# Attention before two MLPs on one core: one or two chunks of p times v made from rounded parts

## The chip, the cores and the metric

The kernel runs on one core of a Trainium2 chip. The metric is device time in microseconds (us) of one execution. Engines are named as in the profile: PE is TensorE (PEld its weight loads), DVE is VectorE, ACT is ScalarE, POOL is GpSimd, SP is SyncE. The time before is the median of three runs, 1681.91 us (1679.18 to 1683.67).

## The reference

Three stages run one after the other on 4 batches of 448 tokens. Attention has 12 heads of 64 elements; two MLPs of width 768 and 3072 follow, the second behind a mix of the tokens through U and V.

```python
q_n, k_n = (rmsnorm(q, g_q), rmsnorm(k, g_k))
scores = 1/sqrt(64) * matmul(q_n, k_n.T)
scores = scores - max(scores, axis=-1)
attn = exp(scores)
attn = attn / (sum(attn, axis=-1) + 1e-09)
x = matmul(attn, v)                       # heads side by side: 4 x 448 x 768
xn = (x - mean) / sqrt(var + 1e-06) * g_ln
x = x + relu(xn @ w_ch1) @ w_ch2          # first MLP
u = x + ((x.T @ U) @ V).T                 # mix of tokens
out = u + relu(u @ w2_ch1) @ w2_ch2       # second MLP
```

## The kernel before

The 48 heads (4 batches of 12) go through `attention` one after the other, two heads of a pair sharing the preparation. The 448 tokens are cut into `NC` = 4 chunks of `CP` = 112. One turn of the main loop is a head, and a turn has four slots, one for each chunk. In a slot every task that is under way makes one step, in the order of `OS`: `sc` (scores of head i, exponentials), `mx` (maxima of head i+2), `pv` (p times v of head i-1), `t1` (transposes of k and q of head i+3, tiles `pk` and `pq`), `t2` (transposes with the maximum, `pt`) and `norm`. Between them run generators in the background: `pre` (norms and rounded parts of q and k, a pair ahead), `pre_v` (loads v), `load_uv`, `scale` (division by the sum of p), `ln_stats` and `ln_apply` (the LayerNorm of a batch whose 12 heads are done; for batches 0 and 1 within attention) and, from head 38 on, `early` and `late` (first weights of the MLP). A scheduler sets the final order on each engine, except for what `pin` holds in its order; every engine then works through its own list without overtaking.

fp32 numbers reach the faster matmul as parts: `F32R` is a rounded fp32 that TensorE takes in one pass, and a product of two split numbers is made as high times high, low times high and high times low. A matmul with plain `F32` operands takes two records in the trace.

`sc` multiplies twice per chunk (L475, L476) into a bank `ps`, and ScalarE writes p, 112x448, as `pf` tile of type F32 (L479). `pv` multiplies p by `vf` (L500): v's 64 columns, and ones behind them up to 128, so that row 64 of the result `po` is the sum of p. VectorE copies the 65 rows that are wanted (L514). The constant `NX` = 4 = `NC` makes all four chunks F32; the branches for rounded parts exist but are not taken, and `pre_v` ends after its two loads of `vf`.

In `mx` VectorE reduces each chunk of scores to its maxima straight from a PSUM bank (L450). Seven banks of tag "ps" go round among `ps`, `pm`, `po` and the transposes. `pre` on GpSimd: multiplication by the norm's factors (L300, twice), low part of k (`kk`, L305), low part of q (`ql`, L308), and the gains (`later`, L287). `kk` of a pair is read by `pk` of `t1` (L428). LayerNorm on GpSimd: L184 and L219 subtract the mean, L215 makes the low part; on VectorE: L163 sums, L181, L222; `scale` multiplies at L555.

Of the kernel before, what the change touches and what calls it, by code (L numbers as in the profile page):

```python
# [8 lines left out]
F32 = mybir.dt.float32  # L9
F32R = mybir.dt.float32r  # L10
# [3 lines left out]
AF = mybir.ActivationFunctionType  # L14
ALU = mybir.AluOpType
AX = mybir.AxisListType

B, H, S, D = 4, 12, 448, 64
P = 128
CP = 112  # L20
NC = S // CP
DM = H * D
DFF = 4 * DM
KD = DM // P
# [6 lines left out]
NWF = 5  # L31
NP0 = 2
EPS = 1e-6
NX = 4
OS = "smpabn"
QW = D + 2
HL = 8
PVY = (0, 1, 2)
# [5 lines left out]
def f32(ap):  # L44
    return ap.bitcast(F32)


def build(tc, qkv, gg, g_ln, w1a, w2a, w1b, w2b, u_in, v_in, out):
    nc = tc.nc
    V, A, PL, PE = nc.vector, nc.scalar, nc.gpsimd, nc.tensor  # L50
    with ExitStack() as es:
# [9 lines left out]
        def bank(name, tag=None):  # L61
            cnt[0] += 1
            tag = tag or banks["tag"]
            return banks["pool"].tile([P, 512], F32, tag=tag, name=f"{name}{cnt[0]}", bufs=banks[tag])
# [40 lines left out]
        v4 = const([4 * R, S], F32R, "v4")  # L105

        def load_ggt(tp):
            gsb = tp.tile([CP, 2, D], F32, tag="gsb", name="gsb")
            nc.scalar.dma_start(gsb, gg)
            ggt = tp.tile([CP, D], F32, tag="ggt", name="ggt")  # L110
            V.scalar_tensor_tensor(ggt, gsb[:, 0, :], 1.0 / D ** 0.5, gsb[:, 1, :], ALU.mult, ALU.mult)
            return ggt
# [22 lines left out]
        x = [xpool.tile([P, KD, S], F32, tag=f"x{b}", name=f"x{b}") for b in range(B)]  # L135
        xh = [npool.tile([P, KD, S], F32R, tag=f"xh{j}", name=f"xh{j}") for j in range(2)]
        xl = [npool.tile([P, KD, S], F32R, tag=f"xl{j}", name=f"xl{j}") for j in range(2)]
# [4 lines left out]
        def pin(ins):  # L142
            return tc.keep_in_program_order(ins) if pins[0] else ins
# [82 lines left out]
        def attention(ap, ep, ep2, early, late):  # L226
            NH = B * H
            NP = NH // 2
            kks, vfs, vhs, vls, a2s = [], [], [], [], []
            st = {}  # L230
# [13 lines left out]
            pre_load(0)  # L244
            side["ln"] = bank("ln", "ln")
            ggt = load_ggt(ap)
            identr = ap.tile([CP, CP], F32R, tag="identr", name="identr")
            pin(V.tensor_copy(identr, ident[:CP, :CP]))
# [2 lines left out]
                PE.matmul(warm[:, :P], ones_m, ones_m, start=True, stop=True)  # L251
            later = ap.tile([CP, D], F32, tag="later", name="later")
            for i in range(2):
                for lst, nm, dt, one in ((vfs, "vf", F32, 1.0), (vhs, "vh", F32R, 1.0), (vls, "vl", F32R, 0.0)):
                    n = NX if nm == "vf" else NC - NX
                    if n == 0:
                        lst.append(None)
                        continue
                    t = ap.tile([CP, 2, n, P], dt, tag=f"{nm}{i}", name=f"{nm}{i}")
                    PL.memset(f32(t[:, :, :, D:P]), one)  # L260
                    lst.append(t)
            for i in range(NA2):
                t = ap.tile([P, S], F32R, tag=f"a2{i}", name=f"a2{i}")
                PL.memset(f32(t[D:QW, :]), 1.0)
                a2s.append(t)
            qls = []
            for i in range(3):
                t = ep.tile([CP, 2 * NC, QW], F32R, tag=f"ql{i}", name=f"ql{i}")
# [133 lines left out]
            def pre_v(pr):  # L402
                b, hp = divmod(pr, H // 2)
                v = qkv[b, hp, :, 2].rearrange("p (j c) d -> p j c d", j=2)
                for j in range(2):
                    ins = (nc.scalar if pr else nc.sync).dma_start(vfs[pr % 2][:, j, :, 0:D], v[:, j, 0:NX])
                    if pr:
                        pin(ins)
                if NX == NC:
                    return  # L410
                vr = ap.tile([CP, 2, NC - NX, D], F32, tag="vr", name=f"vr{pr}", bufs=2)
                nc.sync.dma_start(vr, v[:, :, NX:])
                yield
                yield
                yield
                vh, vl = vhs[pr % 2], vls[pr % 2]
                for j in range(2):
                    A.copy(vh[:, j, :, 0:D], vr[:, j])
                yield
                for j in range(2):  # L420
                    PL.tensor_tensor(vl[:, j, :, 0:D], vr[:, j], f32(vh[:, j, :, 0:D]), ALU.subtract)

            def t1(n):
                pr, j = divmod(n, 2)
# [43 lines left out]
            def sc(n):  # L468
                a1, bq, a2 = st.pop(("ab", n))
                t = st.pop(("t2", n))  # L470
                st["p", n] = ps = []
                for c in range(NC):
                    pb = bank("ps")
                    cs = slice(c * CP, (c + 1) * CP)
                    PE.matmul(pb[:CP, :S], a1[:, cs], bq, start=True, stop=False)  # L475
                    PE.matmul(pb[:CP, :S], a2[:QW, cs], t[:QW], start=False, stop=True)  # L476
                    if c < NX:
                        p = ap.tile([CP, S], F32, tag="pf", name=f"p{n}_{c}", bufs=NX + 2)
                        A.activation(p, pb[:CP, :S], AF.Exp)  # L479
                        ps.append(p)  # L480
                    else:
                        p = ap.tile([CP, S], F32, tag="p", name=f"p{n}_{c}", bufs=2)
                        ph = ap.tile([CP, S], F32R, tag="ph", name=f"ph{n}_{c}", bufs=NC - NX + 1)
                        pl = ap.tile([CP, S], F32R, tag="pl", name=f"pl{n}_{c}", bufs=NC - NX + 1)
                        A.activation(p, pb[:CP, :S], AF.Exp)
                        V.tensor_copy(ph, p)
                        PL.tensor_tensor(pl, p, f32(ph), ALU.subtract)
                        ps.append((ph, pl))
                    if c < NC - 1:
                        yield  # L490

            def pv(n):
                pr, j = divmod(n, 2)
                ps = st.pop(("p", n))
                vf, vh, vl = vfs[pr % 2], vhs[pr % 2], vls[pr % 2]
                po = bank("po")
                st["po", n] = po
                for c in range(NC):
                    if c < NX:
                        PE.matmul(po[:, :S], vf[:, j, c, :], ps[c], start=(c == 0), stop=(c == NC - 1))  # L500
                    else:
                        ph, pl = ps[c]
                        PE.matmul(po[:, :S], vh[:, j, c - NX, :], ph, start=(c == 0), stop=False)
                        PE.matmul(po[:, :S], vl[:, j, c - NX, :], ph, start=False, stop=False)
                        PE.matmul(po[:, :S], vh[:, j, c - NX, :], pl, start=False, stop=(c == NC - 1))
                    if c in PVY:
                        yield

            def norm(n):
# [56 lines left out]
            for i in range(-3 - T1, NH + 2):  # L566
                def ok(n):
                    return 0 <= n < NH
                if i == -3 - T1:
                    start = first_two()  # L570
# [13 lines left out]
                if i - 2 in (H, 2 * H, 3 * H):  # L584
                    b = (i - 2) // H - 1
# [29 lines left out]
        bufs, held, rings, ready = {}, {}, {}, {}  # L615
# [890 lines left out]
```

## Time and profile before

| | us |
|---|---|
| three runs, median | 1681.91 |
| profiled execution | 1675.09 |
| its span | 1673.3 |
| PE busy | 1661.3 |
| DVE, ACT, POOL busy | 1203.5, 1000.5, 1051.1 |

The profiled execution is a run of its own, 1.8 us longer than its span, and shorter than the median of the three timed runs. The first matmul of the MLPs starts at 338.3 us; before that lies attention. Matmuls are pipelined and their ends are modelled: of matmuls in a row, the distances of their starts tell more than one's length, and a busy PE isn't yet a PE at its peak. A window view gives for each engine the busy time in a stretch.

### The profile page before, as it was taken

What the parts mean: (1) busy time and instruction counts of PE and PEld (TensorE: products, weight loads), DVE (VectorE), ACT (ScalarE), POOL (GpSimd) and SP (SyncE); (2) the same over time, 40 slices, a digit from 0 to 9 for tenths busy, and PEclk for the clock granted to TensorE, in tenths of its full rate; (3) what the DMA queues carried; (4) which work ended last, traced back from release to release, by engine and by line L of the source; (5) the groups of instructions that cost most, each with busy time, mean ns of one, the idle gap of its engine ahead of it and who ended that gap; (6) DMA issues with size and microseconds to landing.
All of it is one profiled execution on the core that took longest, in us unless ns stands there. A gap on an engine that the chain in (4) does not pass through costs nothing.

```text
span 1673.3 us, 24654 instructions
## 1 busy us (share of the span) xinstructions
PE 1661.3 (99%) x8223; PEld 1460.3 (87%) x8223; DVE 1203.5 (72%) x1913; ACT 1000.5 (60%) x2098; POOL 1051.1 (63%) x924
## 2 busy tenths in 40 slices
PE   8999999999999999999999999999999999999999
PEld 6666666689999999999999999999999999999998
DVE  6657777879897887866767686657667854565665
ACT  7877888867878876544544455444445534454541
POOL 5446767559767787755655687555555655776752
PEclk8999999999999999999999999999999999999999
DMA  3435444766755566544445427565657463444432
GB/s 98 117 83 128 121 117 136 205 223 207 236 178 174 185 207 202 190 139 131 152 136 159 157 85 255 190 221 176 226 189 250 166 207 118 147 151 123 150 124 76
DMA packets 134430, 273.39 MB, mean 163 GB/s; under 512 B 37280, under 2 KB 57664, under 8 KB 134304
## 3 DMA queue, kind: packets, MB, share of 16 engines
q1 hardware_dynamic: 112252, 265.24, 49.8%
q10 hardware_dynamic: 22052, 6.59, 1.7%
q8 instruction: 65, 1.06, 0.3%
q14 instruction: 61, 0.50, 0.1%
HBM read 178.80 MB, written 81.96 MB: 156 GB/s over the span
## 4 chain that ended last, share of the span: by engine, by line
PE 94%; DVE 2%; DMA 1%; POOL 1%; issue 1%; ACT 1%; SPq 0%; POOLq 0%; DVEq 0%; ACTq 0%
PE bank L1111 35%; PE bank L1289 33%; PE po L500 7%; PE bank L1233 6%; PE ps L475 2%; PE b L1111 2%; PE pm L449 2%; PE ps L476 2%; PE b L1233 2%; PE t L978 1%; PE pk L428 1%; PE pq L436 1%; PE xt L968 1%; PE pt L463 0%; DMA xl<-rs 0%
## 5 line engine op out<-in xcount | busy, mean ns | idle before, releaser
L1289 PE MATMUL bank<-h,w 128*128 128x448 f32 x2655 | 586.1, 366 | 0.0
L1289 PEld LDWEIGHTS bank<-h,w 128*128 128x128 f32 x2655 | 498.3, 188 | 38.3 <-issue 0.4
L1300 DVE TENSOR_TENSOR x<-x,bank 128x448 f32<-128x448 f32 x450 | 275.8, 616 | 188.8 <-PE bank L1289 183.8
L1111 PE MATMUL bank<-xh,w 128*128 128x448 f32 x1158 | 330.5, 367 | 0.0
L785 POOL TENSOR_TENSOR w<-wf,w 128x384 fp32r<-128x384 f32 x201 | 222.7, 1119 | 133.1 <-ACT w L784 131.6
L785 POOL TENSOR_TENSOR w<-s,w 128x384 fp32r<-128x384 f32 x151 | 173.4, 1151 | 152.4 <-ACT w L784 149.1
L1111 PE MATMUL bank<-T,w 128*128 128x448 f32 x1134 | 251.9, 367 | 0.0
L1111 PEld LDWEIGHTS bank<-xh,w 128*128 128x128 f32 x1158 | 217.2, 188 | 17.5 <-issue 0.7
L1111 PEld LDWEIGHTS bank<-T,w 128*128 128x128 f32 x1134 | 212.3, 188 | 16.4
L1111 PE MATMUL bank<-xl,w 128*128 128x448 f32 x579 | 211.9, 366 | 0.0
L784 ACT CAST w<-s 128x384 fp32r<-128x384 f32 x151 | 77.1, 515 | 174.5 <-PE bank L1111 160.5
L500 PE MATMUL po<-p,vf 112*128 112x448 f32 x384 | 175.6, 539 | 0.2 <-DVE m L450 0.2
L450 DVE TENSOR_REDUCE m<-pm 112x1 f32<-112x448 f32 x192 | 118.5, 619 | 64.4 <-PE pm L449 63.8
L784 ACT CAST w<-wf 128x384 fp32r<-128x384 f32 x201 | 101.5, 514 | 100.6 <-PE bank L1111 81.7
L83 DVE SCALAR_TENSOR_TENSOR wf<-wf,raw 128x384 uint32<-128x384 uint32 x180 | 135.2, 757 | 13.2 <-ACT raw L71 5.3
L785 POOL TENSOR_TENSOR w<-raw,w 128x384 fp32r<-128x384 f32 x72 | 81.9, 1154 | 57.1 <-ACT w L784 57.0
L1111 PEld LDWEIGHTS bank<-xl,w 128*128 128x128 f32 x579 | 108.9, 188 | 8.6
L79 ACT ACTIVATE wf<-raw 128x384 f32<-128x384 f32 x180 | 99.3, 553 | 27.5 <-DMA raw<-in_w2a 11.2
L479 ACT ACTIVATE p<-ps 112x448 f32<-112x448 f32 x192 | 104.5, 546 | 4.3 <-PE ps L476 2.1
L1103 DVE SCALAR_TENSOR_TENSOR h<-tm,h 128x448 fp32r<-128x448 f32 x103 | 99.7, 968 | 2.9 <-ACT h L1102 2.2
L71 ACT ACTIVATE raw<-raw 128x384 uint32<-128x384 uint8 x180 | 100.0, 558 | 0.0
L475 PE MATMUL ps<-bq,a 128*112 128x448 f32 x192 | 98.6, 513 | 0.0
(263 smaller groups left out, 2891.1 us busy)
## 6 DMA issues: line engine op xcount, KB each, us to landing
wd<-wf SPq DMA_DIRECT2D x94, 384.0 KB
ws<-w SPq DMA_DIRECT2D x84, 384.0 KB
w<-ws SPq DMA_DIRECT2D x84, 384.0 KB
wf<-wd SPq DMA_DIRECT2D x51, 384.0 KB
raw<-wd SPq DMA_DIRECT2D x48, 384.0 KB
raw<-in_w1b SPq DMA_DIRECT2D x48, 384.0 KB
raw<-in_w2b SPq DMA_DIRECT2D x48, 384.0 KB
raw<-in_w2a SPq DMA_DIRECT2D x44, 384.0 KB
```

The lines of the kernel that those rows point to most:

```text
L71: A.activation(r[:, :, 0], r.bitcast(U8).rearrange("p n (t q) -> p n t q", t=2)[:, :, 0, 3], AF.Copy, scale=1.0 / 32, bias=-31.0 / 64)
L83: V.scalar_tensor_tensor(f, f, 3, r[:, :, 0], ALU.logical_shift_left, ALU.bitwise_or)
L450: V.tensor_reduce(m[:, c:c + 1], pm[:CP, :S], AX.X, ALU.max)
L475: PE.matmul(pb[:CP, :S], a1[:, cs], bq, start=True, stop=False)
L479: A.activation(p, pb[:CP, :S], AF.Exp)
L500: PE.matmul(po[:, :S], vf[:, j, c, :], ps[c], start=(c == 0), stop=(c == NC - 1))
L784: job(A, 520, lambda: A.copy(form(key)[0], src()), ins, ("hi",) + key, [key])
L785: job(PL, 1100, lambda: PL.tensor_tensor(form(key)[1], src(), f32(form(key)[0]), ALU.subtract), [("hi",) + key], key, rel=rel)
L1111: PE.matmul(out[:, :S], wt[:, k, :], xt[:, k, :], start=(first and n == 0), stop=(last and n == 8), skip_group_check=True)
L1233: PE.matmul(at(*to)[:, :S], wt[:, e, :], xt, start=(m in "13" and n == 0), stop=(n == 2), skip_group_check=True)
L1289: PE.matmul(at(*key)[:, :S], wt[:, e % 3, :], t, start=(n == 0), stop=(n == 3 * G - 1))
L1300: V.tensor_tensor(x[b][:, e, :], x[b][:, e, :], at(*key)[:, :S], ALU.add)
```

## The change

`NX` goes, and four numbers come: `H0, H2, H1, NV = 4, 14, 38, 2`. `parts(n)` says how many chunks of head n are made from rounded parts: none in heads 0 to 3, two in heads 4 to 13, one in heads 14 to 37, none from 38 on. All four chunks of v stay in `vf` as F32, now 66 columns wide (`QW`), and `vh` and `vl` hold the high and low part of the first one or two. For such a chunk VectorE writes the high part of p as a maximum over an axis of one element (`ph`), GpSimd subtracts (`pl`), two slots after the exponential; `pv` takes the F32 chunks first and the rounded ones last, with three matmuls each. `ph` and `pl` live in slices of `xh[1]` and `xl[1]` up to head 23 and in the MLP's weight ring `w` from 24 on. The first load `gsb` goes to a corner of `x[3]`.

```diff
@@ -31,7 +31,7 @@
 NWF = 5
 NP0 = 2
 EPS = 1e-6
-NX = 4
+H0, H2, H1, NV = 4, 14, 38, 2
 OS = "smpabn"
 QW = D + 2
 HL = 8
@@ -105,7 +105,7 @@
         v4 = const([4 * R, S], F32R, "v4")
 
         def load_ggt(tp):
-            gsb = tp.tile([CP, 2, D], F32, tag="gsb", name="gsb")
+            gsb = x[B - 1][:CP, 0, :2 * D].rearrange("p (j d) -> p j d", j=2)
             nc.scalar.dma_start(gsb, gg)
             ggt = tp.tile([CP, D], F32, tag="ggt", name="ggt")
             V.scalar_tensor_tensor(ggt, gsb[:, 0, :], 1.0 / D ** 0.5, gsb[:, 1, :], ALU.mult, ALU.mult)
@@ -251,14 +251,23 @@
                 PE.matmul(warm[:, :P], ones_m, ones_m, start=True, stop=True)
             later = ap.tile([CP, D], F32, tag="later", name="later")
             for i in range(2):
-                for lst, nm, dt, one in ((vfs, "vf", F32, 1.0), (vhs, "vh", F32R, 1.0), (vls, "vl", F32R, 0.0)):
-                    n = NX if nm == "vf" else NC - NX
-                    if n == 0:
-                        lst.append(None)
-                        continue
-                    t = ap.tile([CP, 2, n, P], dt, tag=f"{nm}{i}", name=f"{nm}{i}")
-                    PL.memset(f32(t[:, :, :, D:P]), one)
+                for lst, nm, dt, n, one in ((vfs, "vf", F32, NC, 1.0), (vhs, "vh", F32R, NV, 1.0), (vls, "vl", F32R, NV, 0.0)):
+                    t = ap.tile([CP, 2, n, QW], dt, tag=f"{nm}{i}", name=f"{nm}{i}")
+                    PL.memset(f32(t[:, :, :, D:QW]), one)
                     lst.append(t)
+            spare = [xx[1][:CP, k, :] for xx in (xh, xl) for k in range(KD)]
+            ring_w = [t.rearrange("p a b c -> p (a b c)")[:CP, :S] for t in bufs["w"]]
+            taken = [0]
+
+            def parts(n):
+                return 0 if n < H0 else NV if n < H2 else 1 if n < H1 else 0
+
+            def homes(n):
+                pool = spare if n < 2 * H else ring_w
+                i = taken[0] % len(pool)
+                taken[0] += 2
+                return pool[i], pool[i + 1]
+
             for i in range(NA2):
                 t = ap.tile([P, S], F32R, tag=f"a2{i}", name=f"a2{i}")
                 PL.memset(f32(t[D:QW, :]), 1.0)
@@ -402,23 +411,20 @@
             def pre_v(pr):
                 b, hp = divmod(pr, H // 2)
                 v = qkv[b, hp, :, 2].rearrange("p (j c) d -> p j c d", j=2)
+                vf, vh, vl = vfs[pr % 2], vhs[pr % 2], vls[pr % 2]
                 for j in range(2):
-                    ins = (nc.scalar if pr else nc.sync).dma_start(vfs[pr % 2][:, j, :, 0:D], v[:, j, 0:NX])
+                    ins = (nc.scalar if pr else nc.sync).dma_start(vf[:, j, :, 0:D], v[:, j])
                     if pr:
                         pin(ins)
-                if NX == NC:
+                m = parts(2 * pr)
+                if m == 0:
                     return
-                vr = ap.tile([CP, 2, NC - NX, D], F32, tag="vr", name=f"vr{pr}", bufs=2)
-                nc.sync.dma_start(vr, v[:, :, NX:])
-                yield
-                yield
-                yield
-                vh, vl = vhs[pr % 2], vls[pr % 2]
-                for j in range(2):
-                    A.copy(vh[:, j, :, 0:D], vr[:, j])
-                yield
-                for j in range(2):
-                    PL.tensor_tensor(vl[:, j, :, 0:D], vr[:, j], f32(vh[:, j, :, 0:D]), ALU.subtract)
+                yield
+                yield
+                yield
+                A.copy(vh[:, :, :m, 0:D], vf[:, :, :m, 0:D])
+                yield
+                PL.tensor_tensor(vl[:, :, :m, 0:D], vf[:, :, :m, 0:D], f32(vh[:, :, :m, 0:D]), ALU.subtract)
 
             def t1(n):
                 pr, j = divmod(n, 2)
@@ -469,41 +475,44 @@
                 a1, bq, a2 = st.pop(("ab", n))
                 t = st.pop(("t2", n))
                 st["p", n] = ps = []
+                st["hl", n] = hl = []
+
+                def part(c):
+                    ph, pl = homes(n)
+                    V.tensor_reduce(ph, ps[c].unsqueeze(2), AX.X, ALU.max)
+                    PL.tensor_tensor(pl, ps[c], f32(ph), ALU.subtract)
+                    hl.append((ph, pl))
+
                 for c in range(NC):
+                    if 0 <= c - 2 < parts(n):
+                        part(c - 2)
                     pb = bank("ps")
                     cs = slice(c * CP, (c + 1) * CP)
                     PE.matmul(pb[:CP, :S], a1[:, cs], bq, start=True, stop=False)
                     PE.matmul(pb[:CP, :S], a2[:QW, cs], t[:QW], start=False, stop=True)
-                    if c < NX:
-                        p = ap.tile([CP, S], F32, tag="pf", name=f"p{n}_{c}", bufs=NX + 2)
-                        A.activation(p, pb[:CP, :S], AF.Exp)
-                        ps.append(p)
-                    else:
-                        p = ap.tile([CP, S], F32, tag="p", name=f"p{n}_{c}", bufs=2)
-                        ph = ap.tile([CP, S], F32R, tag="ph", name=f"ph{n}_{c}", bufs=NC - NX + 1)
-                        pl = ap.tile([CP, S], F32R, tag="pl", name=f"pl{n}_{c}", bufs=NC - NX + 1)
-                        A.activation(p, pb[:CP, :S], AF.Exp)
-                        V.tensor_copy(ph, p)
-                        PL.tensor_tensor(pl, p, f32(ph), ALU.subtract)
-                        ps.append((ph, pl))
+                    p = ap.tile([CP, S], F32, tag="pf", name=f"p{n}_{c}", bufs=NC + 2)
+                    A.activation(p, pb[:CP, :S], AF.Exp)
+                    ps.append(p)
                     if c < NC - 1:
                         yield
 
             def pv(n):
                 pr, j = divmod(n, 2)
-                ps = st.pop(("p", n))
+                ps, hl = st.pop(("p", n)), st.pop(("hl", n))
                 vf, vh, vl = vfs[pr % 2], vhs[pr % 2], vls[pr % 2]
                 po = bank("po")
                 st["po", n] = po
-                for c in range(NC):
-                    if c < NX:
-                        PE.matmul(po[:, :S], vf[:, j, c, :], ps[c], start=(c == 0), stop=(c == NC - 1))
+                m = len(hl)
+                for i in range(NC):
+                    c = (i + m) % NC
+                    if c >= m:
+                        PE.matmul(po[:QW, :S], vf[:, j, c, :], ps[c], start=(i == 0), stop=(i == NC - 1))
                     else:
-                        ph, pl = ps[c]
-                        PE.matmul(po[:, :S], vh[:, j, c - NX, :], ph, start=(c == 0), stop=False)
-                        PE.matmul(po[:, :S], vl[:, j, c - NX, :], ph, start=False, stop=False)
-                        PE.matmul(po[:, :S], vh[:, j, c - NX, :], pl, start=False, stop=(c == NC - 1))
-                    if c in PVY:
+                        ph, pl = hl[c]
+                        PE.matmul(po[:QW, :S], vh[:, j, c, :], ph, start=False, stop=False)
+                        PE.matmul(po[:QW, :S], vl[:, j, c, :], ph, start=False, stop=False)
+                        PE.matmul(po[:QW, :S], vh[:, j, c, :], pl, start=False, stop=(i == NC - 1))
+                    if i in PVY:
                         yield
 
             def norm(n):
```

Both orders below are of the kernel as built; line numbers of the changed kernel are its own (L509 and L512 to L514 are the matmuls of `pv`, L482 is `ph`, L483 `pl`, L427 `vl`; L455, L491, L492, L442 are what L449, L475, L476 and L436 were).

On PE, the last two slots of a turn (head 9 before, head 8 after: `ps` scores, `pm` for maxima, `po` p times v). Before:

```order
L475 MATMUL ps_1317<-bq_1090,a_9_1048 112x448
L476 MATMUL ps_1317<-t_9_1229,a_353 112x448
L449 MATMUL pm_1322<-a_11_1207,bq_1249 112x448
L500 MATMUL po_1281<-p_2_1238,vf_349 128x448
L436 MATMUL pq_1326<-identr,qd_1187 128x112 x4
L475 MATMUL ps_1336<-bq_1090,a_9_1048 112x448
L476 MATMUL ps_1336<-t_9_1229,a_353 112x448
L449 MATMUL pm_1341<-a_11_1207,bq_1249 112x448
L500 MATMUL po_1281<-p_3_1255,vf_349 128x448
```

After:

```order
L491 MATMUL ps_1278<-bq_1030,a_8_973 112x448
L492 MATMUL ps_1278<-t_8_1182,a_364 112x448
L455 MATMUL pm_1283<-a_10_1160,bq_1207 112x448
L512 MATMUL po_1241<-xh_87,vh_356 66x448
L513 MATMUL po_1241<-xh_87,vl_358 66x448
L514 MATMUL po_1241<-xh_87,vh_356 66x448
L442 MATMUL pq_1289<-identr,qd_1050 128x112 x4
L491 MATMUL ps_1299<-bq_1030,a_8_973 112x448
L492 MATMUL ps_1299<-t_8_1182,a_364 112x448
L455 MATMUL pm_1304<-a_10_1160,bq_1207 112x448
L512 MATMUL po_1241<-xh_87,vh_356 66x448
L513 MATMUL po_1241<-xh_87,vl_358 66x448
```

The place of `po` in a slot is the same; one F32 matmul has become three rounded ones.

On DVE, the end of the sums for the LayerNorm of batch 0, in turns 18 and 19 (`ln_xs` sums over x, `m` maxima, `xh_87` the slices that hold `ph`). Before:

```order
L163 TENSOR_REDUCE ln_xs<-x_82 128x112
L450 TENSOR_REDUCE m_2022<-pm_2047 112x1
L163 TENSOR_REDUCE ln_xs<-x_82 128x112
L289 TENSOR_REDUCE ln_305<-qsq_1_1999 112x8
L450 TENSOR_REDUCE m_2022<-pm_2068 112x1
L163 TENSOR_REDUCE ln_xs<-x_82 128x112
L291 TENSOR_SCALAR ss_1929<-ln_305 112x16
L450 TENSOR_REDUCE m_2022<-pm_2086 112x1
L514 COPY u_2119<-po_2026 65x448
```

After:

```order
L163 TENSOR_REDUCE ln_xs<-x_82 128x112
L456 TENSOR_REDUCE m_2139<-pm_2164 112x1
L163 TENSOR_REDUCE ln_xs<-x_82 128x112
L298 TENSOR_REDUCE ln_305<-qsq_1_2112 112x8
L482 TENSOR_REDUCE xh_87<-p_0_2136 112x448
L456 TENSOR_REDUCE m_2139<-pm_2187 112x1
L163 TENSOR_REDUCE ln_xs<-x_82 128x112
L300 TENSOR_SCALAR ss_2040<-ln_305 112x16
L456 TENSOR_REDUCE m_2139<-pm_2205 112x1
L456 TENSOR_REDUCE m_2227<-pm_2228 112x1
L523 COPY u_2240<-po_2143 65x448
```

One reduction `ph` of each head stands among the maxima, and the copy `u` is one maximum later.

On POOL, the preparation of a pair beside the LayerNorm of batch 0, turns 21 and 22 (`kk` low part of k, `ql` of q, `ln_d` minus mean). Before:

```order
L219 TENSOR_TENSOR ln_d_2646<-x_82,ln_mu 128x448
L308 TENSOR_TENSOR ql_359<-raw_0_1802,qd_2180 112x8x64
L287 TENSOR_TENSOR raw_0_1977<-raw_0_1977,later 112x512
L219 TENSOR_TENSOR ln_d_2552<-x_82,ln_mu 128x448
L300 TENSOR_TENSOR raw_1_1979<-raw_1_1979,sy_2094 112x512
L300 TENSOR_TENSOR raw_0_1977<-raw_0_1977,sy_2094 112x512
L219 TENSOR_TENSOR ln_d_2572<-x_82,ln_mu 128x448
L219 TENSOR_TENSOR ln_d_2594<-x_82,ln_mu 128x448
L219 TENSOR_TENSOR ln_d_2608<-x_82,ln_mu 128x448
L305 TENSOR_TENSOR kk_2360<-raw_1_1979,kk_2360 112x8x64
```

After:

```order
L483 TENSOR_TENSOR xh_87<-p_0_2313,xh_87 112x448
L317 TENSOR_TENSOR ql_366<-raw_0_1903,qd_2306 112x8x64
L296 TENSOR_TENSOR raw_0_2088<-raw_0_2088,later 112x512
L483 TENSOR_TENSOR xl_89<-p_0_2409,xl_89 112x448
L219 TENSOR_TENSOR ln_d_2699<-x_82,ln_mu 128x448
L309 TENSOR_TENSOR raw_1_2090<-raw_1_2090,sy_2215 112x512
L309 TENSOR_TENSOR raw_0_2088<-raw_0_2088,sy_2215 112x512
L219 TENSOR_TENSOR ln_d_2719<-x_82,ln_mu 128x448
L219 TENSOR_TENSOR ln_d_2743<-x_82,ln_mu 128x448
L427 TENSOR_TENSOR vl_358<-vf_354,vh_356 112x2x64
L219 TENSOR_TENSOR ln_d_2759<-x_82,ln_mu 128x448
L314 TENSOR_TENSOR kk_2496<-raw_1_2090,kk_2496 112x8x64
```

Two `pl` and one `vl` stand ahead of `kk` here; one more `vl` lies a few rows earlier, among the squares of the LayerNorm.

## Rows read from the trace of the kernel before

**Rows 1.** The page: busy time by engine, and the chain that ended last.
```profile
PE 1661.3 (99%) x8223; PEld 1460.3 (87%) x8223; DVE 1203.5 (72%) x1913; ACT 1000.5 (60%) x2098; POOL 1051.1 (63%) x924
...
PE 94%; DVE 2%; DMA 1%; POOL 1%; issue 1%; ACT 1%; SPq 0%; POOLq 0%; DVEq 0%; ACTq 0%
```
**Rows 2.** The chain in order of time, pieces: start us, us, what.
```profile
133.29 3.92 DMA xl<-rs
...
338.81 18.24 PE bank L1111 x90
```
**Rows 3.** Busy time by stretch: length, then each engine (instructions), PE clock, DMA.
```profile
53.35:66.46 13.11, 13.11 (x66) 8.87 (x65) 10.76 (x26) 11.20 (x29) 5.71 (x5) 1.00 0.42 119
66.46:111.58 45.12, 45.12 (x227) 31.37 (x225) 26.80 (x54) 34.88 (x82) 19.73 (x18) 1.00 0.39 99
...
130.92:150.29 19.37, 18.97 (x90) 12.51 (x89) 17.45 (x31) 12.93 (x34) 8.68 (x7) 1.00 0.52 122
152.38:171.52 19.14, 19.14 (x96) 13.27 (x95) 14.52 (x29) 17.97 (x41) 19.14 (x18) 1.00 0.29 72
...
211.69:231.35 19.66, 19.66 (x99) 13.44 (x97) 19.18 (x33) 15.03 (x37) 8.87 (x7) 1.00 0.67 165
237.34:257.24 19.90, 19.90 (x100) 13.76 (x99) 14.29 (x30) 17.52 (x43) 19.90 (x19) 1.00 0.41 102
```
**Rows 4.** Instructions in time: start us, us, engine, line, [idle before <- releaser].
```profile
143.29 0.37 PE L449 MATMUL pm<-a,bq 128*112 128x448 f32 x1
...
146.37 0.60 DVE L450 TENSOR_REDUCE m<-pm 112x1 f32<-112x448 f32 x1
...
147.02 0.17 PEld L449 LDWEIGHTS pm<-a,bq 128*112 128x112 f32 x1 [0.45 <-DVE m L450]
```
**Rows 5.** Instructions in time on PE, end of attention and first MLP.
```profile
334.13 1.67 PE L500 MATMUL po<-p,vf 112*128 112x448 f32 x4
...
336.39 2.42 PE L500 MATMUL po<-p,vf 112*128 112x448 f32 x6
...
339.66 0.37 PE L1111 MATMUL bank<-xl,w 128*128 128x448 f32 x1
...
340.27 0.37 PE L1111 MATMUL bank<-xl,w 128*128 128x448 f32 x1
```
**Rows 6.** Groups on DVE, 111 to 272 us: busy us, mean ns, idle before.
```profile
L450 DVE TENSOR_REDUCE m<-pm 112x1 f32<-112x448 f32 x97 | 59.7, 617 | 29.5 <-PE pm L449 28.9
L289 DVE TENSOR_REDUCE ln<-qsq 112x8 f32<-112x512 f32 x23 | 15.8, 687 | 0.7 <-ACT qsq L281 0.2
L514 DVE COPY u<-po 65x448 f32<-65x448 f32 x24 | 14.7, 612 | 0.5
L163 DVE TENSOR_REDUCE ln_xs<-x 128x112 f32<-128x672 f32 x8 | 10.6, 1340 | 0.0
```
**Rows 7.** Instructions in time: POOL and what stands beside it.
```profile
134.37 3.21 POOL L300 TENSOR_TENSOR raw<-raw,sy 112x512 f32<-112x512 f32 x2 [3.49 <-DVE sy L149]
135.52 1.15 DVE L555 TENSOR_TENSOR x<-x,xl 128x448 f32<-128x448 f32 x2
...
148.64 2.04 POOL L300 TENSOR_TENSOR raw<-raw,sy 112x512 f32<-112x512 f32 x2 [4.88 <-DVE sy L149]
...
153.48 4.47 POOL L184 TENSOR_TENSOR ln_sq<-x,ln_mu 128x448 f32<-128x448 f32 x4
...
170.24 1.28 POOL L305 TENSOR_TENSOR kk<-raw,kk 112x512 fp32r<-112x512 f32 x1
...
173.68 0.80 PE L428 MATMUL pk<-identr,kk 112*128 112x112 f32 x4
...
249.27 1.28 POOL L305 TENSOR_TENSOR kk<-raw,kk 112x512 fp32r<-112x512 f32 x1
...
252.56 0.80 PE L428 MATMUL pk<-identr,kk 112*128 112x112 f32 x4
```
**Rows 8.** A group on ACT, 46 to 112 us.
```profile
L431 ACT CAST a<-pk 128x448 fp32r<-128x448 f32 x10 | 5.3, 533 | 2.0 <-PE pk L428 1.6
```

## The prediction

> **What bounds the kernel now.** I read the page first, then the chain of waits, then the busy time of each engine by stretch, then single rows. TensorE is busy for 99% of the span, and 94% of the chain that ended last is TensorE [rows 1]. From 338.81 us on the chain is one matmul behind the other [rows 2], so the MLP part only passes on what attention hands it, and attention is where the change works. Seven light heads take 45.12 us there, 6.45 us each, with TensorE never idle, VectorE busy for 26.80 and GpSimd for 19.73 of it [rows 3]: in light heads only TensorE counts. The same view shows stretches where another engine is full too: GpSimd for 19.14 of 19.14 us (from 152.38) and for 19.90 of 19.90 us (from 237.34), VectorE for 19.18 of 19.66 us (from 211.69). In a fourth (from 130.92) VectorE has 17.45 of 19.37 us, and there TensorE does wait for it: scores whose matmul began at 143.29 us were reduced at 146.37 us, 2.7 us after it ended, and TensorE's next pm had to wait 0.45 us for a bank [rows 4]. So two things matter: what TensorE saves, and what the change adds in those four stretches.
>
> **What TensorE saves.** Two records make one fp32 chunk of p times v. Four records in a row last 1.67 us and six last 2.42 us [rows 5], so one costs (2.42 - 1.67)/2 = 0.375 us and a chunk 0.75 us. A rounded chunk takes three passes at the rate of the MLP's matmuls: their group of three that begins at 339.66 us is followed by the next at 340.27 us, 0.61 us for three. Each chunk that is moved saves 0.14 us. Ten heads move two chunks and 24 heads one, 44 in all: 44 x 0.14 = 6.2 us. The passes also load 66 columns of weights instead of 128; loads run beside the matmuls, so I count nothing. Were it the load that sets the pitch of 0.61/3 = 0.203 us, the 132 new passes could at best fall to 448 columns at 2.4 GHz, 0.187 us: 132 x 0.016 = 2.1 us more, the upper bound of the gain.
>
> **What it adds on VectorE.** 44 reductions over an axis of one element, 112x448 in and 448 out; no row shows that form. The nearest: 448 elements to one take 617 ns, 512 to eight 687 ns, and a copy with 448 out 612 ns [rows 6]. On the far side stands L163, 672 elements to 112 outputs in 1340 ns. By the first two rows an element costs (687 - 617)/64 = 1.1 ns, so L163 has 1340 - 617 - 224 x 1.1 = 477 ns that its elements don't explain; as a price of its 111 further outputs that is 4.3 ns each, and 448 outputs would cost 617 + 447 x 4.3 = 2.5 us. I take 0.62 us, by the copy, which also writes 448, and because L163 alone reads with a stride of 448 elements. The Trainium skill (SBUF — State Buffer, Door 1: The DMA port swizzle) says that an access that crosses into a new 16-byte line pays a penalty, which would put L163's excess on its stride; no run here separates the two, and by that rule 0.62 us stays.
>
> In heads 4 to 13 two reductions, 1.24 us, come to VectorE's 26.80/7 = 3.8 us of a head that shrinks to 6.17 us: covered. The tightest place there are heads 5 and 6, where U and V are converted (10.76 of 13.11 us [rows 3]); with four reductions more, 13.2 us stand against two heads of 6.2 us. The next head absorbs the lag of under 1 us, and I price the waiting at 0.3 us. From 130.92 to 150.29 us VectorE gets three reductions; one finds idle time, since the multiplications there wait for a transfer of 3.92 us [rows 2]. The other two, 1.2 us, go on a queue that already stops TensorE: 1.2 us lost. From 211.69 to 231.35 us come three, 1.9 us, against 0.5 us of idle time, and TensorE arrives some 0.4 us earlier, but the lag before is smaller: I take 0.9 us, between 0 and 1.9.
>
> **What it adds on GpSimd.** 44 subtractions pl like L184, four of which in a row took 4.47 us [rows 7], 1.12 us each, and 17 vl of 128 or 256 elements. By L184's 448 elements and the kk's 512 in 1.28 us an element costs 2.5 ns, so a vl 0.3 to 0.65 us. They stand in one queue with the preparation of q and k. A light pair of heads gives GpSimd 2 x 19.73/7 = 5.6 us; four pl and a vl make it 10.8 of 12.3 us: full, not over. From 152.38 us on, GpSimd has no idle time, and the order puts two pl and two vl ahead of the kk of 170.24 us: 2 x 1.12 + 2 x 0.3 = 2.9 us later. This kk ended at 171.52 us and its reader, the transposes pk, began at 173.68 us: 2.2 us of slack, less some 0.3 us by which TensorE comes earlier. Lost: 2.9 - 1.9 = 1.0 us. From 237.34 us on, one pl and one vl are ahead of the kk that ends at 250.55 us, 1.5 us, and pk comes at 252.56 us, 2.0 us after it: nothing lost.
>
> **What I count at nothing.** ScalarE makes 17 copies vh of 128 or 256 elements, each under the 0.53 us of 448 [rows 8], in heads where it is busy for 34.88 of 45.12 us [rows 3]. A copy waits for v's transfer, and the exponentials queue behind it; a transfer like it took 3.92 us [rows 2], about the distance between issue and copy. p is read most of a head later, so a wait of up to 1 us is covered; without that cover the copies of the crowded heads might add 2 us together. Turning the chunks round (2, 3, 0, 1 or 1, 2, 3, 0) has chunk 3 read up to two slots earlier, still after its exponential. v's transfers keep number and bytes, gsb its size.
>
> Sum: -6.2 + 0.3 + 1.2 + 0.9 + 1.0 = -2.8 us. The profiled execution took 1675.09 us, so 1672.3 us; it lies 6.8 us under the median of the runs, 1681.91 us, to which the same difference gives **1679.1 us**.
>
> **Rivals.**
> B, the cover holds everywhere. For it: GpSimd was full for 19 us twice, and TensorE was busy all through both [rows 3]. Against it: VectorE's lag of 2.7 us did cause waits. -6.2 us, 1675.7 us; with the faster passes 1673.6 us.
>
> C, slower: GpSimd becomes the bound in heads 14 to 37. Its instructions stretch where VectorE multiplies two tensors: two L300 took 3.21 us at 134.37 us and 2.04 us at 148.64 us, 1.17 us more, which is the 1.15 us of VectorE's two multiplications within the first [rows 7]. The skill (SBUF — State Buffer, Who interferes with whom) has this as a rule: a VectorE instruction with two SBUF inputs and a GpSimd one that reads SBUF contend, the second fully blocks, and tensor_reduce is free of it; the trace agrees, 1.17 against 1.15 us. If four of the new subtractions meet such a multiplication (4 x 0.6 = 2.4 us) and kk comes late by all that is added ahead of it in three crowded places (2.9, 1.5 and as much again as the larger, with no slack left: 7.3 us), it loses 9.7 us there and 1.5 us at VectorE against 6.2: +5.0 us, 1686.9 us. It decides once kk comes over 2 us later than now.
>
> D, the reduction is paid by output, 2.5 us. Then VectorE needs 3.8 + 5.0 = 8.8 us of a head of 6.2 us ten times, 26 us over, and in the 24 other heads, most of them fuller, at least 3.8 + 2.5 against 6.3: +26 us or more, 1708 us. Only L163 speaks for it.
>
> E, the change doesn't do what it says: passes behind fp32 matmuls start late, a rounded chunk costs 0.70 us. It saves 2.2 and loses 3.4 us: 1683.1 us.
>
> **How the numbers follow.** Forecast 0.46 (its own range 1676.0 to 1682.0), B 0.31, C 0.13, D 0.03, E 0.07. A measurement can tell about 0.3%, 5.0 us, from no change. Faster by more: three quarters of B and a fifth of the forecast, 0.33. Slower by more: half of C, and D, 0.10. The rest, 0.57, is the same. The range: B with faster passes, 1673.6, less 1.6 us for scatter (the runs before lie from 1679.18 to 1683.67), 1672; upward to half of C, 1687.
>
> **What would show it.** Light heads of 6.45 - 0.28 = 6.17 us, and 6.3 us where one chunk moves; the new reduction near 0.62 us, the subtraction near 1.12 and not 1.7 us; longer waits of TensorE for VectorE's reductions near 150 and 230 us, a new wait of pk for GpSimd's kk near 170 us, none in light heads; the MLP part as long as before. The forecast is wrong if the light heads keep 6.45 us (E), if VectorE is full in heads 4 to 13 (D), or if TensorE waits nowhere longer than before (B).

## The result and the profile after

The changed kernel takes 1688.9 us (median of 11 runs, 1686.79 to 1695.78) against 1679.83 us of the kernel before (median of 11): the ratio on record is 1.0061, 95% interval [1.0044, 1.0078] (the two medians alone give 1.0054). It is slower by about 0.6%, where 0.2% faster was forecast, and 1.9 us above the range. The runs of one kernel can fall into two groups some 7 us apart at the same granted clock (of 29 later runs of the kernel before, 23 took 1674.4 to 1678.7 us and six 1681.3 to 1683.9), which no trace here explains, so differences of 0.1 or 0.2% between versions are at the edge of what the runs can tell. The profiled execution took 1686.79 us with a span of 1685.0; before, the span was 1673.3.

The page of the changed kernel: busy time, and the chain that ended last.

```profile
PE 1659.9 (99%) x8267; PEld 1443.6 (86%) x8267; DVE 1233.4 (73%) x1957; ACT 1003.2 (60%) x2115; POOL 1105.1 (66%) x989
...
PE 89%; DVE 3%; DMA 3%; POOL 2%; ACT 2%; issue 1%; SPq 0%; ACTq 0%; POOLq 0%; DVEq 0%
```

Against [rows 1] TensorE's share of the chain fell from 94% to 89%; its busy time is nearly the same. The MLPs are not to blame: from their first matmul to the last record of a matmul they take 1331.6 us, before 1331.5. The loss lies ahead of it, and a table by turn shows where (a turn is the distance from a head's first matmul of scores to the next head's, read from the profiled runs, and has the number of its head; `pv` of head n runs in turn n+1; sums in us):

```
turns    before  after  e1     e2     e3     e4     e5     e10    e11
5-14      64.7   63.8   63.3   64.8   63.4   62.9   66.1   65.0   66.7
15-20     40.6   39.4   39.8   41.9   39.9   39.3   41.4   40.9   43.1
21-23     20.1   21.7   20.1   21.6   21.7   19.6   20.1   20.0   20.4
24         6.5    7.8    6.4    7.8    6.3    6.3    6.4    6.4    7.8
26         7.2    8.5    7.2    8.6    7.9    7.5    7.7    7.4    8.4
28         6.4   11.2    6.4   11.2    6.3    6.3    6.4    6.4   11.0
29-31     19.7   21.2   19.5   20.2   20.8   21.2   20.6   20.2   19.6
34-35     13.7   15.4   13.6   17.0   15.4   13.8   14.0   13.6   15.7
39-46     51.7   52.5   53.2   51.9   52.1   52.0   51.9   55.2   52.6
```

What TensorE was to save is there: turns 8 to 11 take 6.13 us on average against 6.45, undisturbed turns with one chunk 6.29. But one turn, 28, loses 4.7 us by itself. VectorE, GpSimd and TensorE in that turn of the changed kernel (start us, us, engine and line, idle time before and what ended it), with one earlier row of the same line at the top:

```profile
117.77 0.19 DVE L544 SCALAR_TENSOR_TENSOR ss<-ss,sy 128x42 f32<-128x42 f32 x1
...
207.08 4.60 DVE L544 SCALAR_TENSOR_TENSOR ss<-ss,sy 128x42 f32<-128x42 f32 x1
211.60 0.61 DVE L523 COPY u<-po 65x448 f32<-65x448 f32 x1
...
213.48 0.60 DVE L482 TENSOR_REDUCE w<-p 112x448 fp32r<-112x448 f32 x1
```
```profile
206.81 1.17 POOL L483 TENSOR_TENSOR w<-p,w 112x448 fp32r<-112x448 f32 x1
207.91 2.06 POOL L309 TENSOR_TENSOR raw<-raw,sy 112x512 f32<-112x512 f32 x2
209.91 0.47 POOL L427 TENSOR_TENSOR vl<-vf,vh 112x128 fp32r<-112x128 f32 x1
210.33 1.29 POOL L314 TENSOR_TENSOR kk<-raw,kk 112x512 fp32r<-112x512 f32 x1
214.16 1.13 POOL L483 TENSOR_TENSOR w<-p,w 112x448 fp32r<-112x448 f32 x1 [2.55 <-DVE w L482]
```
```profile
208.87 0.36 PE L492 MATMUL ps<-t,a 66*112 66x448 f32 x1
212.26 0.45 PE L455 MATMUL pm<-a,bq 128*112 128x448 f32 x1 [3.04 <-DVE u L523]
```

L544 adds and multiplies 42 numbers per partition of two tiles in SBUF; at 117.77 us the same line took 0.19 us. Here it takes 4.60 us and ends at 211.68 us, 0.07 us after GpSimd's kk, the last instruction of a run without a gap. From here on such an instruction, whose record is long while GpSimd works, is called held. GpSimd then pauses only because its next pl needs a reduction ph (L482) that itself is queued behind L544. Behind L544 stands the copy u, which frees the bank that TensorE's pm needs. TensorE pauses, and the pause costs more than its length: the granted clock falls.

```profile
206.94:208.97 2.03, 2.03 (x12) 1.30 (x10) 2.03 (x2) 0.84 (x3) 2.03 (x3) 1.00 0.24 57
208.97:212.26 3.29, 0.26 (x2) 0.00 (x0) 3.29 (x4) 2.87 (x5) 2.64 (x4) 1.00 0.00 0
212.26:215.80 3.54, 3.54 (x11) 2.11 (x12) 2.44 (x7) 0.87 (x2) 1.64 (x2) 0.55 0.19 39
```

The columns are those of [rows 3]. After 3.29 us with almost nothing to do, TensorE runs for the next 3.54 us at a mean clock of 0.55, so most of the time at the lower of its two levels, 1.2 GHz. The same hold, smaller, makes turn 24 long:

```profile
177.66 2.92 DVE L147 TENSOR_TENSOR ln_xs<-ln_acc 128x448 f32<-128x448 f32 x1 [1.10 <-ACT ln_acc L198]
```
```profile
176.53 2.06 POOL L309 TENSOR_TENSOR raw<-raw,sy 112x512 f32<-112x512 f32 x2
178.53 1.16 POOL L483 TENSOR_TENSOR xl<-p,xl 112x448 fp32r<-112x448 f32 x1
179.62 0.48 POOL L427 TENSOR_TENSOR vl<-vf,vh 112x128 fp32r<-112x128 f32 x1
181.94 1.91 POOL L314 TENSOR_TENSOR kk<-raw,kk 112x512 fp32r<-112x512 f32 x1 [1.84 <-ACT kk L312]
```

L147 (y times y, both in SBUF) took 0.63 us before. Now it starts within GpSimd's run, is overtaken twice by GpSimd's next instruction, and ends 0.5 us after the run does.

### The profile page after: what moved, and what is told of

The parts are those of the page before. It is cut to its first block, busy times and chain, and to the rows that moved or that the text cites. A ratio compares the mean times of both kernels' runs of the same rounds, so it can differ in the third digit from the quotient of the medians.

```text
span 1685.0 us, 24899 instructions
## 1 busy us (share of the span) xinstructions
PE 1659.9 (99%) x8267; PEld 1443.6 (86%) x8267; DVE 1233.4 (73%) x1957; ACT 1003.2 (60%) x2115; POOL 1105.1 (66%) x989
## 4 chain that ended last, share of the span: by engine, by line
PE 89%; DVE 3%; DMA 3%; POOL 2%; ACT 2%; issue 1%; SPq 0%; ACTq 0%; POOLq 0%; DVEq 0%
PE bank L1120 35%; PE bank L1298 33%; PE bank L1242 6%; PE po L509 3%; PE b L1120 2%; PE b L1242 2%; PE ps L491 2%; PE pm L455 2%; PE ps L492 1%; DMA vf<-in_qkv 1%; DMA raw<-in_qkv 1%; DVE m L456 1%; PE t L987 1%; PE xt L977 1%; DVE ln_xs L163 1%
## 5 line engine op out<-in xcount | busy, mean ns | idle before, releaser
L509 PE MATMUL po<-p,vf 112*66 112x448 f32 x296 | 136.0, 542 | 0.0
L1161 DVE TENSOR_TENSOR tm<-tm,bank 128x448 f32<-128x448 f32 x102 | 63.0, 617 | 46.4 <-PE bank L1120 45.7
```

The lines of the kernel that those rows point to most:

```text
L509: PE.matmul(po[:QW, :S], vf[:, j, c, :], ps[c], start=(i == 0), stop=(i == NC - 1))
```

## Experiments

Theory P: a VectorE instruction with two operands in SBUF is held while GpSimd works without a gap, and the new instructions close GpSimd's gaps. Theory Q: GpSimd's own results come late. Rival V: VectorE's reductions cost the time. Rival S: the loss lies in what all heads share (66 columns, the order of the chunks). Ratios are against the kernel before, run again beside each group of experiments on the same chip; turns are of the profiled run, one for each version. In the cuts of code `...` stands for lines left out.

**e1 and e2: the two halves of the change.**

```diff
-H0, H2, H1, NV = 4, 14, 38, 2
+H0, H2, H1, NV = 4, 14, 14, 2      # e1
+H0, H2, H1, NV = 14, 14, 38, 2     # e2
```

> Two chunks in heads 4 to 13, none elsewhere (20 of the 44). Theory Q (GpSimd's queue is too full from head 20 on, and what reads from it comes late): the heads from 15 on keep the periods of before, the turns 5 to 14 take 63.8 us against 64.7, and the time is about 1 us below before, ratio 0.999. Rival S (the loss lies in what all heads share: 66 columns, the order of the chunks, the scheduler's new order): the heads from 15 on lose 5 us or more, ratio above 1.002.

> One chunk in heads 14 to 37, none elsewhere (24 of the 44). Theory Q: nearly the whole loss is here, turns 15 to 38 take about 170 us against 159.7, and the time is 9 to 12 us above before, ratio about 1.006. Rival S or a loss that is carried from the early heads: turns 15 to 38 lose under 5 us, ratio below 1.003.

e1: 0.9992 [0.9983, 1.0002]; from turn 15 on nothing is lost up to 38. e2: 1.0081 [1.0065, 1.0097], with the same 11.17 us in turn 28. The loss is in heads 14 to 37, and it needs nothing from the heads ahead. S falls.

**e3: the held instructions get one operand from PSUM.** `side["ln"]` is a bank of PSUM; z takes the place of y in the two instructions behind the first one as well.

```diff
+                z = side["ln"][:, :n] if n == H * S // P else y
...
-                pin(A.activation(y, s, AF.Ln, bias=tiny))
-                pin(A.activation(y, y, AF.Exp, scale=-1.0))
+                pin(A.activation(z, s, AF.Ln, bias=tiny))
+                pin(A.activation(z, z, AF.Exp, scale=-1.0))
-                pin(V.scalar_tensor_tensor(s, s, 1e-9, y, ALU.add, ALU.mult))
+                pin(V.scalar_tensor_tensor(s, s, 1e-9, z, ALU.add, ALU.mult))
...
+            if pool:
+                pin(A.activation(t, y, AF.Square))
-            rsqrt_newton(y, a, t, a if pool and b < 2 else y)
+            rsqrt_newton(y, a, t, a if pool and b < 2 else y, square=not pool)
```

> The changed kernel, with one operand of VectorE's L544 to L546 in PSUM, and ScalarE instead of VectorE squaring y before L148, so that neither reads two tensors from SBUF. Theory P (VectorE's instruction with two operands in SBUF is held until GpSimd's gapless run of instructions ends): L544 of 4.60 us falls to 0.2 us, turn 28 from 11.2 to about 6.5 us, turn 24 from 7.8 to about 6.6, and the time is some 6 us below the changed kernel, ratio to before about 1.002. Theory Q alone: VectorE's long instruction is idle time that other waits fill as well, turn 28 stays over 9 us, and the ratio stays at 1.005 to 1.007.

0.9994 [0.9982, 1.0006], median 1676.9 us: the loss against the kernel before is gone, though the 6.8 us that TensorE was to save do not show. P had expected some 6 us less than the changed kernel takes, from turns 24 and 28 (now both 6.3 us). The span is 9.6 us shorter, 6.4 us of it in these two turns; the rest lies in turns 12 and 26 (0.8 and 0.6), in 39 to 46 (0.4) and just ahead of the MLPs (1.5), and no held instruction was shown behind it. The changed kernel's L544 is L547 here:

```profile
204.67 0.19 DVE L547 SCALAR_TENSOR_TENSOR ss<-ss,ln 128x42 f32<-128x42 f32 x1
```

**e4: no pl.**

```diff
-                    PL.tensor_tensor(pl, ps[c], f32(ph), ALU.subtract)
...
-                        PE.matmul(po[:QW, :S], vh[:, j, c, :], pl, start=False, stop=(i == NC - 1))
+                        PE.matmul(po[:QW, :S], vh[:, j, c, :], ph, start=False, stop=(i == NC - 1))
```

> The changed kernel without GpSimd's 44 subtractions pl; the third matmul takes the high part again, so the product with the low part of p is left out. The passes on TensorE and VectorE's reductions are the same. Theories Q and P: with 50 us less on GpSimd both its late results and its long runs go, the turns 15 to 38 take under 160 us, and the time is 2 to 5 us below before, ratio about 0.998. Rival V (VectorE's 44 reductions cost the time): still 5 us or more above before, ratio over 1.003.

0.9995 [0.9981, 1.0010]; turns 15 to 38 take 158.8 us. V falls as the cause of most of the loss, though the gain over the kernel before is less than the expected 0.998. The waits of turns 21, 22, 24, 28 and 34 are gone, so they come from GpSimd's load; 29 to 31 stay at 21.2 us, so those don't come from pl, and e7 below puts them on VectorE's reductions.

**e5, e10, e11: parts of the load without TensorE's saving.** In all three `pv` takes its four chunks as F32 (`m = 0`); e5 and e10 make no vh and vl either. e5 keeps of the rest only a subtraction on GpSimd, e10 only the reductions, e11 everything.

```diff
-                m = len(hl)
+                m = 0                                             # all three
...
-                    V.tensor_reduce(ph, ps[c].unsqueeze(2), AX.X, ALU.max)      # not in e5
-                    PL.tensor_tensor(pl, ps[c], f32(ph), ALU.subtract)          # not in e10
+                    PL.tensor_tensor(pl, ps[c], ps[c], ALU.subtract)            # e5
```

> Of the whole change only GpSimd's load: at the same 44 places GpSimd subtracts p from itself into the buffer of pl, which nobody reads; all chunks of p times v stay F32, and there are no reductions, no vh and no vl. Theory P with Q (the time is lost by GpSimd's queue, by late results and by VectorE's instructions that its gapless runs hold): 8 to 14 us above before, ratio 1.005 to 1.008, with L544 or the L147 of a LayerNorm over 1.5 us long. Rival V (VectorE's reductions are needed for the loss): within 3 us of before, ratio under 1.002.

> Of the whole change only VectorE's load: the 44 reductions ph are made and nobody reads them; no pl, no vh, no vl, all chunks of p times v F32. Theory: VectorE's queue costs in turns 17 to 19 and 30, 31, some 2 us, ratio 1.001, with no held L544 or L147. Rival V (the reductions carry most of the loss): 6 us or more, ratio over 1.003.

> The changed kernel in all but TensorE's passes: ph, pl, vh and vl are made, and all chunks of p times v are multiplied as F32 chunks of 66 columns. If TensorE's saving is real and adds to the rest, this is 6 to 7 us slower than the changed kernel, ratio to before 1.009 to 1.011. If the saving is eaten by the waits anyway (TensorE arrives earlier and waits longer): like the changed kernel or at most 3 us above, ratio 1.006 to 1.008.

e5: 1.0036 [1.0023, 1.0048], less than expected: L147 was held (2.02 us), the first instruction of `scale` only 0.94, and turns 24 and 28 stay at 6.4 us: these holds cost no time. The load is also lighter than the changed kernel's, since the stand-in reads one tensor, takes 0.93 us at the median for pl's 1.15, and has no vl beside it. e10: 1.0027 [1.0011, 1.0042], more than expected and not without holds: in turn 40 (8.22 us against 6.45 before), where no reduction is made, three of VectorE's instructions each lasted to the end of one GpSimd instruction of the old work:

```profile
289.86 1.06 DVE L543 SCALAR_TENSOR_TENSOR ss<-ss,sy 128x42 f32<-128x42 f32 x1 [0.59 <-ACT sy L541]
290.95 1.23 DVE L544 TENSOR_TENSOR ss<-ss,sy 128x42 f32<-128x42 f32 x1
292.21 1.19 DVE L545 SCALAR_TENSOR_TENSOR sy<-sy,ss 128x42 f32<-128x42 f32 x1
```

e11: 1.0080 [1.0068, 1.0092], with L544 at 4.42 us and turn 28 at 10.96 us again. By the ratios GpSimd's load alone costs 0.36% and VectorE's alone 0.27%, both with vh and vl 0.80%; these intervals leave room for a plain sum. The turns 15 to 38 say more: they lose 2.4, 1.6 and 12.2 us, so in these runs it is far from a sum, though e5's load is the lighter one, and the long hold came only with all of it, not with either half. From e11 to the changed kernel TensorE's passes bring 0.19%, 3 us, of the 6.8 due, with intervals that overlap; by the turns it is 3.0 of 3.1 us in 5 to 14 and 2.1 of 3.7 in 15 to 38, by the spans 4.2 us. That is near the second answer: part of the saving is eaten by waits, and how much is known only to within some us.

**e6: e3's edit in the kernel before.** The diff is e3's.

> The kernel before with the edit of e3 alone. There GpSimd's queue has idle time beside L544 to L546 and L147, which take 0.2 and 0.6 us: theory P expects no difference, ratio 0.999 to 1.001. If the edit of e3 gains time by itself, whatever GpSimd does, the ratio is 0.996 or less, and e3 says nothing on the change.

0.9989 [0.9978, 1.0000]: hardly anything, so e3's gain is made against what the change brought. It also means that with the same edit in both kernels the change still gains nothing (0.9994 against 0.9989).

**e9: half of e3's edit** (the lines with `z`, not the square).

> The changed kernel with only the first half of e3's edit: an operand of L544 to L546 in PSUM, L147 as it was. Theory P by place: turn 28 falls from 11.2 to under 6.6 us, turn 24 keeps 7.5 to 7.8 us with an L147 of over 2 us; 5 to 7 us below the changed kernel, ratio to before 1.001 to 1.003. If the long waits go or stay by the chance of a new order, and not by the operand's place: turn 24 falls too, or turn 28 stays over 9 us.

1.0021 [1.0012, 1.0029]: turn 28 falls to 6.30 us, turn 24 stays at 7.74. The changed kernel's L544 is L545 here and isn't held, and L147, which keeps its two operands in SBUF, is:

```profile
211.13 0.19 DVE L545 SCALAR_TENSOR_TENSOR ss<-ss,ln 128x42 f32<-128x42 f32 x1
```
```profile
180.07 2.92 DVE L147 TENSOR_TENSOR ln_xs<-ln_acc 128x448 f32<-128x448 f32 x1 [1.08 <-ACT ln_acc L198]
```

In these two places the operand's place decided, and not a new order; this is P's clearest test. Turns 6 and 26 are 2.0 and 1.7 us longer here than in the changed kernel, which stays unexplained.

**e12: a copy for the reduction** (with e3's edit).

```diff
-                    V.tensor_reduce(ph, ps[c].unsqueeze(2), AX.X, ALU.max)
+                    V.tensor_copy(ph, ps[c])
```

> e3 with the high part made by a plain copy on VectorE (SBUF to SBUF) in place of the maximum over an axis of one element. If GpSimd's runs hold only instructions with two operands in SBUF: copies of 0.3 to 0.6 us, none longer, ratio 0.998 to 1.000. If a copy is held as well: copies of 1 us and more beside GpSimd's work, ratio over 1.003.

1.0052 [1.0037, 1.0068], against e3's 0.9994. P as stated is too narrow: a copy has one operand and is held too. Durations by tile in e12 (ns: least, median, longest), and the longest in time:

```profile
L484 DVE CAST xh<-p x15: 375/702/1474, 49.5 to 155.0; 112x448 fp32r<-112x448 f32 x15
L484 DVE CAST xl<-p x15: 376/732/1389, 60.6 to 177.6; 112x448 fp32r<-112x448 f32 x15
L484 DVE CAST w<-p x14: 373/396/4976, 184.5 to 284.9; 112x448 fp32r<-112x448 f32 x14
```
```profile
257.66 4.98 DVE L484 CAST w<-p 112x448 fp32r<-112x448 f32 x1 [1.68 <-ACT p L496]
```

Left alone the copy needs 0.38 us, less than the reduction's 0.61; but 23 of 44 took over 0.7 us, and one lasted through GpSimd's run until 262.38 us and ended at 262.63, in a turn (34) of 13.2 us. Of the 44 reductions of the changed kernel none took over 0.622 us. The Trainium skill (SBUF — State Buffer, Who interferes with whom) has the ports for it: copies and casts can run in a mode that uses the pair shared with GpSimd, a tensor_reduce on trn2 never; the traces agree, 4.98 and 0.62 us at most.

**e7: ScalarE writes the high part** (with e3's edit).

```diff
-                    V.tensor_reduce(ph, ps[c].unsqueeze(2), AX.X, ALU.max)
...
+                    if c < parts(n):
+                        highs[c] = homes(n)
+                        A.activation(highs[c][0], pb[:CP, :S], AF.Exp)
```

> e3 with the high part of p written by a second exponential on ScalarE from the PSUM bank, in place of VectorE's reduction. If VectorE's queue costs what e3 still loses in turns 30 and 31 (0.9 and 0.4 us), these fall to 6.5 us or less and the ratio is 0.998; turns 21 to 23, 34 and 35 (GpSimd's late results) stay. If ScalarE, with 24 us more, becomes late itself: ratio over 1.001, and scores wait for exponentials.

1.0024 [1.0013, 1.0035], the second answer. Turn 30 falls to 6.29 us, so VectorE did cost there (31 keeps 7.05), but turn 5 takes 9.90 us, where ScalarE also converts U and V.

**e8: rounded chunks only in heads with free engines** (with e3's edit).

```diff
+            HALF = [0] * 4 + [2] * 3 + [1] * 3 + [0, 0, 1, 0, 1, 0, 0, 0, 1] + [0] * 5
...
             def parts(n):
-                return 0 if n < H0 else NV if n < H2 else 1 if n < H1 else 0
+                return HALF[n // 2]
```

> e3 with rounded chunks only where no other engine is full: two in heads 8 to 13, one in 14 to 19, 24, 25, 28, 29, 36 and 37, none elsewhere (24 chunks). At 0.155 us each that is 3.7 us; theories P and Q expect nearly all of it, ratio 0.998. If a chunk also costs in light heads, or the rest goes at turn 19: ratio 1.000.

0.9998 [0.9989, 1.0007]. In the profiled run turns 5 to 38 are 2.2 us shorter than before, but 39 to 46 take 54.1 us against 51.7, and what was won is lost there. It goes in turn 42, 8.69 us against 6.45: VectorE's product of x and r waits 3.22 us for r's transfer (1.59 us before), a maximum stands behind it in VectorE's list, and TensorE waits for the maximum.

```profile
295.71 0.62 DVE L569 TENSOR_TENSOR x<-x,r 128x448 f32<-128x448 f32 x1 [3.22 <-DMA r<-rs]
```
```profile
296.93 0.97 PE L513 MATMUL po<-p,vf 112*66 112x448 f32 x2 [1.74 <-DVE m L460]
```

Why the transfer came later is open; e1 and e6 lose 1.4 and 1.5 us in these turns as well. None of the versions is clearly faster than the kernel before.

## Why the prediction was wrong, step by step

The mechanism of TensorE's saving was right: 44 chunks at 0.155 us, 6.8 us for 6.2. The prices of single instructions were right: ph 0.61 us for 0.62 [rows 6], pl 1.17 to 1.23 for 1.12 [rows 7], and D fell. A vl of 256 elements was dearer than its bound of 0.65 us: 0.73 in four cases and 1.11 in one; one of 128 took 0.46. E fell, for the saving came, and B, for the cover didn't hold.

The step that failed is "What it adds on GpSimd". It let GpSimd's load act only through what reads GpSimd's results (kk before pk). The load acts also through what VectorE may not do meanwhile: turns 24 and 28 lose 1.5 and 4.9 us against an undisturbed 6.29, and 44 cheap subtractions turned an L544 of 0.19 us into 4.60. These 6.4 us are the largest part of what the sum lacked and the one that e9 and e3 show; the rest is spread over the terms below. Rival C named the contention, but priced it in one direction only, VectorE stretching GpSimd; its 1686.9 us is near the result by the wrong path, which is luck. The other direction stood in the trace of before, unread. VectorE and GpSimd of the kernel before, turn 28:

```profile
206.99 0.89 DVE L537 SCALAR_TENSOR_TENSOR sy<-sy,ss 128x42 f32<-128x42 f32 x1
```
```profile
206.54 1.28 POOL L305 TENSOR_TENSOR kk<-raw,kk 112x512 fp32r<-112x512 f32 x1 [1.82 <-ACT kk L303]
```

42 numbers in 0.89 us, ending with kk; and ahead of kk the 1.82 us without work in which L535 (205.59 us) had passed. The change filled that gap.

The other steps, by the profiled runs (loss = turn less before, plus the saving due):

- Heads 5 and 6: 0.3 us predicted, 13.8 - 13.1 + 0.6 = 1.3 lost.
- VectorE at 130 to 150 us: 1.2 predicted, nothing lost (turns 17 to 19 are 0.8 us shorter, 0.5 of it due).
- VectorE at 211 to 231 us: 0.9 predicted, 2.0 lost in turns 29 to 31; at the upper end of the bounds. Without the reductions (e7) 0.4 is lost there, without pl (e4) all of it stays.
- kk at 152 to 171 us: 1.0 predicted, 2.0 lost in turns 21 to 23. In turns 34 and 35 nothing was predicted and 2.0 lost. e4 puts most of both on GpSimd. The wait that was forecast, of pk for kk, is there, but small: pk's weights wait 0.64 us at 173.05 us. More is lost ahead of kk, which the text didn't look at: ScalarE's copy L312 reads what L309 on GpSimd multiplied, it waits 1.7 us in turn 22 and again in turn 34, and exponentials stand behind it.

```profile
173.05 0.40 PEld L434 LDWEIGHTS pk<-identr,kk 112*128 112x128 f32 x4 [0.64 <-POOL kk L314]
```
```profile
167.07 0.62 ACT L312 CAST kk<-raw 112x512 fp32r<-112x512 f32 x1 [1.71 <-POOL raw L309]
...
256.10 0.62 ACT L312 CAST kk<-raw 112x512 fp32r<-112x512 f32 x1 [1.65 <-POOL raw L309]
```
```profile
255.04 2.03 POOL L309 TENSOR_TENSOR raw<-raw,sy 112x512 f32<-112x512 f32 x2
```

- Turn 26: 1.5 us lost, not in the sum. VectorE waits 2.2 us for GpSimd's ln_d.
- "What I count at nothing": from 90 us on five copies vh waited for v's transfer, 6.1 us together. One of them began at 99.75 us after a wait of 1.96 us; its transfers had been issued at 93.0 and 93.4 us, so they took over 6 us, where the text had 3.92 from another transfer. The exponential stood behind the copy, and turn 12 lost 0.8 us. The text gave 2 us without the cover.

```profile
99.75 0.41 ACT L425 CAST vh<-vf 112x256 fp32r<-112x256 f32 x1 [1.96 <-DMA vf<-in_qkv]
100.06 0.54 ACT L494 ACTIVATE p<-ps 112x448 f32<-112x448 f32 x1
```

- The MLP part is as long as forecast, but its first matmul waits 1.5 us for the last copy u, and turns 39 to 46 lose 0.7 us. Neither was in the sum.

Together some 18 us lost against 6.8 saved, about the 11.7 us by which the spans differ.

## What to carry to other kernels

Before work is put on GpSimd, list VectorE's instructions that read two tensors from SBUF, and its copies, near that place: what counted here was less GpSimd's busy time than its gaps. Where such a gap closes, give VectorE one operand in PSUM, or a form that isn't held; here the high part of p as a maximum over an axis of one element is a copy that was never held. And an engine's durations of before are worth sorting for outliers: here one instruction at five times its usual length (0.89 us for 0.19) named a contention that the new load multiplied.

## What the runs showed of the hardware that was not expected

- A hold can last through several GpSimd instructions: L544's 4.60 us reached past four ends of GpSimd instructions to the fifth, a copy's 4.98 us past as many; in e10 the wait ended with the first each time. In the longest cases it ended 0.07 to 0.5 us after the end of GpSimd's gapless run. What decides whether VectorE gets in between two instructions wasn't tried and stays open.
- A pause of TensorE of 3 us was followed by 3.5 us at a granted clock of 0.55: the turn lost 4.9 us.
- The copy from SBUF to SBUF of 448 numbers took 0.38 us undisturbed, the reduction to the same 448 numbers 0.61.
